# Linear attention and a bilinear FFN on one Trainium2 core: first stores over three queues, bulk loads and conversions reordered in the opening

## The chip, the core and the metric

The kernel runs on one NeuronCore of one Trainium2 chip. A core has TensorE (matmuls, results in PSUM), VectorE, ScalarE, GpSimd and SyncE, each with an instruction stream of its own that runs in program order, and 16 DMA engines that are fed through queues. SyncE, ScalarE and GpSimd can all issue DMAs. The metric is the device time of one execution in microseconds (us); the kernel before has a median of 604.79 us over 4 runs (604.5 to 605.08).

## What is computed

The reference has two stages. The first is a gated linear attention over 4 batches, 8 heads, 768 tokens and 48 channels; the second is a bilinear feed-forward block over its 3072 tokens of 384 channels:

```python
f = 1.0 / (1.0 + np.exp(-f_logit))
for t in range(S):
    state = f[:, :, t, :, None] * state + np.einsum('bhd,bhe->bhde', k[:, :, t], v[:, :, t])
    y[:, :, t] = np.einsum('bhd,bhde->bhe', q[:, :, t], state)
...
a = x @ w_a
b = x @ w_b
return (a * b @ w_out).astype(np.float32)
```

x is y with its heads side by side. w_a and w_b are 384 x 1536 and w_out is 1536 x 384; all three come as 64-bit floats, the rest as 32-bit.

## The kernel before

**Units and blocks.** The attention is done in 16 units. A unit is one batch, one half of its tokens (384) and four heads; units 0 and 1 are the two head groups of the first half of batch 0, units 2 and 3 those of its second half. Two units make one block of 384 tokens, whose y, turned so that channels lie on partitions, is the tile xT (three channel tiles of 128, numbered by kt). Unit 0 of a block fills channels 0 to 191, unit 1 the rest, so each unit's y goes to xT in five DMAs (`stores_of`, L533 to L556), since heads of 48 channels straddle the tiles of 128. Three sets of input tiles serve the units in turn (`sets[u % 3]`).

**One unit.** `front_parts` (L296 to L341) turns the gates into running products: two sigmoids on ScalarE (L306, L309), an affine step on GpSimd (L312), then on VectorE two scans of f (L316), a check (`hold`, L319), a reciprocal (L324), six scans of the inverse (L329), and the products of k and q with them (L333). Then come, on TensorE, `scores` (L387), `turn` (transposes of k, L411), `within` (L484), `gains` (L435) and `across` (L505); on VectorE `mask` (L400), five or six `carry` steps (L462, L464) and, in a first half, `hand_on` (L473). `within` and `across` add y up in two PSUM banks; `out_of_bank` (L514 to L524) copies it to SBUF in three parts: one copy for bank 0 and two, of 48 rows each, for bank 1. `stored` issues the five DMAs and, from unit 2 on, the loads of the unit three further on.

**Weights.** The weights are loaded in 20 pieces (`load_weights`, L239), most of 768 KB, and each is turned to 32 bits by `from_double` (L52): ScalarE L58 and L59, GpSimd L60, ScalarE L62 and L63, VectorE L68 and L73. `begin(n)` issues the ScalarE and GpSimd part up to piece n - 1 (half a piece for n.5), `end(n)` VectorE's; from the third piece on, `end` also issues a further piece's load where a buffer comes free. Pieces are counted from 0 here. There are four raw buffers, used in turn, and two early ones.

**The feed-forward block.** `up(blk, ft)` (L578 to L602) multiplies xT of a block with 128 columns of w_b and w_a: for each, channel tiles 0, 1, 2 in turn, six matmuls of 128 x 384, which the trace shows as twelve since a 32-bit matmul is two. `product` (L604) copies b out of PSUM on ScalarE (L610), multiplies on VectorE (L612) and gives the two banks back; there are four such banks.

**Order.** The opening, units 0 to 3 and up(0, 0) to up(0, 4), is written out by hand (L935 to L1064), and each engine runs its instructions in this order. Then follow up(0, 5), up(1, 0) and so on, in a loop that converts the remaining pieces as it goes (L1067 to L1077). From L1080 on a planner lays the steps of the remaining units and of the FFN side by side by costs and due times. The change lies in the opening alone. SyncE issues the loads and most stores there; of the stores of units 0 and 1, unit 0's first two and unit 1's last two are on ScalarE's queue (L545).

**Semaphores of DMAs.** The DMAs of SyncE and ScalarE share eight semaphores; a DMA waits until the one that used its semaphore before has landed. In the trace the stores of units 0 and 1 wait in this way too.

Of the kernel before, what the change touches and what calls it, by code (L numbers as in the profile page):

```python
# [26 lines left out]
R = 64  # L27
SUB = 64
# [108 lines left out]
def by_quotients(ctx, tc, q, k, f_logit, v, moe_w_a, moe_w_b, moe_w_out, out, ident, weights, bad):  # L137
    nc = tc.nc
    B, H, D, S = q.shape
# [4 lines left out]
    NQ = H // 4  # L144
# [7 lines left out]
    FIRST = range(NQ)  # L152
# [46 lines left out]
    def load_unit(u, names="fkqv"):  # L199
        for do in loads_of(u, names):  # L200
            do()
# [37 lines left out]
    def load_weights(n=1):  # L239
        for _ in range(n):  # L240
            if len(raws) == len(todo):
                return
            dst, src, (k, m) = todo[len(raws)]
            raw = dst
            if src.dtype != FP32:

                if len(raws) in EARLY:
                    raw = groups[:, EARLY.index(len(raws))].bitcast(mybir.dt.uint64)
                else:
                    raw = next(raw_places)  # L250
                raw = raw[:, 0:k * m].rearrange("p (k m) -> p k m", k=k)
            nc.sync.dma_start(out=raw, in_=src)
            raws.append(raw)
# [16 lines left out]
    def end(n):  # L270

        while ended[0] < min(n, len(todo)):
            begin(ended[0] + 1)
            next(going[ended[0]], None)
            ended[0] += 1
            if ended[0] > 2 and ended[0] - 1 not in EARLY:
                load_weights()
# [15 lines left out]
    def halves(x):  # L293
        return x.rearrange("p n s -> p (n s)")
# [48 lines left out]
    def front(u):  # L343

        for part in front_parts(u):
            for _, _, do, *args in part:
                do(*args)
            yield
# [5 lines left out]
    def tokens(n, c, p):  # L354

        return slice(n * BLK + c * C + p * SUB, n * BLK + c * C + p * SUB + SUB)

    def each():
        for n in range(2):
            for c in range(NC):  # L360
                yield n, c, (n * NC + c) * SUB
# [13 lines left out]
    def pair_of(x):  # L375

        return [x[:, i] for i in range(2)]

    def scores(u):
        t = sets[u % NSET]  # L380
        qf, kf = halves(t["q"]), halves(t["k"])
        ps = pair_of(home(u))
        for n, c, o in each():
            for h in range(2):
                for p in range(2):
                    r = slice(R * h, R * h + D)
                    nc.tensor.matmul(  # L387
                        ps[h][SUB * p:SUB * p + SUB, o:o + SUB],
                        lhsT=kf[r, tokens(n, c, p)],
                        rhs=qf[r, tokens(n, c, p)],  # L390
                        start=True,
                        stop=True,
                    )
# [9 lines left out]
    def turn(u):  # L403

        kf = halves(sets[u % NSET]["k"])
        live.setdefault(u, {})["kT"] = sb1.tile([128, 2, NC, 128], FP32, tag="kT", name="kT")
        ps = live[u]["turned"] = [ps_f[idle.pop(0)] for _ in range(2)] if u in FIRST else pair_of(away(u))
        for n in range(2):
            for c in range(NC):
                o = n * BLK + c * C  # L410
                nc.tensor.transpose(ps[n][:, c * C:c * C + C], kf[:, o:o + C], ident)  # L411
# [36 lines left out]
    def carried(u, js=range(NJ)):  # L448

        for j in js:  # L450
            if j + 1 < len(live[u]["st"]):
                carry(u, j)
        if js[-1] == NJ - 1:
            give_back(live[u]["turned"])
# [11 lines left out]
    def hand_on(u):  # L466

        if unit(u)[1] == NH - 1:
            return
        before = live[u]["st"][-1]  # L470
        for n in range(2):
            end = products_of_f[u][:, n, BLK - 1:BLK]
            nc.vector.tensor_scalar(before[:, n], before[:, n], end, math.exp(-MIDDLE), ALU.mult, ALU.mult)  # L473

    def within(u):

        t, at = sets[u % NSET], live[u]["at"]
        ps = live[u]["y"] = pair_of(home(u) if u < 2 * NQ else ps_y)
        for n, c, o in each():
            for p in range(2):  # L480
                for h in range(2):
                    r = slice(SUB * p, SUB * p + SUB)
                    e = R * (p ^ h)
                    nc.tensor.matmul(  # L484
                        ps[p][e:e + D, o:o + SUB],
                        lhsT=t["v"][r, n, c, h * D:h * D + D],
                        rhs=at[r, h, o:o + SUB],
                        start=o == 0,
                        stop=True,
                        skip_group_check=True,  # L490
                    )

    def across(u):

        b, half, qd = unit(u)
        qf, st, ps = halves(sets[u % NSET]["q"]), live[u]["st"], live[u]["y"]

        for n, c, o in reversed(list(each())) if half or u in FIRST else each():
            for p in reversed(range(2)) if u in FIRST else range(2):
                j = 2 * c + p  # L500
                if j == half == 0:
                    continue
                for h in range(2):
                    r, e = slice(R * h, R * h + D), R * (p ^ h)
                    nc.tensor.matmul(  # L505
                        ps[p][e:e + D, o:o + SUB],
                        lhsT=st[j][r, n],
                        rhs=qf[r, tokens(n, c, p)],
                        start=False,
                        stop=True,  # L510
                        skip_group_check=True,
                    )

    def out_of_bank(u, part):  # L514

        if not part:
            if u == NQ - 1:

                live[u]["y_sb"] = groups[:, 2 * NTG - 1, PIECE:].rearrange("r (o p m) -> r o p m", p=2, m=SUB)
            else:  # L520
                live[u]["y_sb"] = sb1.tile([128, 2 * NC, 2, SUB], FP32, tag="y", name="y")
        p, e, r, rows = ((0, 0, 0, 128), (1, R, 0, D), (1, 0, R, D))[part]
        copy = nc.vector.tensor_copy if u in FIRST and part > u else nc.scalar.copy
        copy(live[u]["y_sb"][r:r + rows, :, p], live[u]["y"][p][e:e + rows, 0:BLK].rearrange("r (o m) -> r o m", m=SUB))  # L524

    def stored(u):
# [6 lines left out]
    def stores_of(u):  # L533

        b, half, qd = unit(u)
        blk = b * NH + half

        def begin():
            if qd == 0:
                xT[blk] = sb2.tile([128, NKT, BLK], FP32, tag="xT", name="xT")  # L540
            live.pop(u - NQ, None)

        def store(n, h, kt, p, row, w):
            y = live[u]["y_sb"].rearrange("r (n c) p m -> r n (c p m)", n=2)
            queue = nc.scalar if u in FIRST and n == u else nc.sync  # L545
            queue.dma_start(out=xT[blk][p:p + w, kt], in_=y[row:row + w, n])

        yield begin
        for n in range(2):
            for h in range(2):  # L550
                ch, row, left = (4 * qd + 2 * n + h) * D, R * h, D
                while left:
                    kt, p = divmod(ch, 128)
                    w = min(left, 128 - p)
                    yield partial(store, n, h, kt, p, row, w)
                    ch, row, left = ch + w, row + w, left - w  # L556
# [378 lines left out]
    with tc.manual_schedule():  # L935
# [6 lines left out]
                eng.memset(sets[u][n], 30.0 if n == "f" else 0.0)  # L942
        for ps in (ps_x, ps_y):
            nc.scalar.copy(ps[:, :, 0:BLK], zero.unsqueeze(1).broadcast_to((128, 2, BLK)))
        fronts = [front(u) for u in range(2 * NQ)]

        def y_of(u):
            for part in range(3):
# [15 lines left out]
        load_weights(2)  # L964
        load_unit(2, "k")
        load_unit(2, "q")
        load_unit(2, "v")
        load_unit(3, "f")
        load_weights()
        for _ in range(3):  # L970
            next(fronts[0])
        begin(1)
# [8 lines left out]
        turned(1)  # L981
        mask(0)
        scores(1)
        next(fronts[2])
        begin(2.5)
        carried(0, range(4))
        within(0)
# [3 lines left out]

        carried(1, range(1))
        carried(0, range(4, 5))
        within(1)
        gains(1, range(NC - 1, NC))
        across(0)
# [9 lines left out]
        end(2)  # L1006
        for u in FIRST:
            carried(u, range(5, NJ))
            hand_on(u)


        load_unit(3, "k")
        load_unit(3, "q")
        load_unit(3, "v")
        load_weights()
        up(0, 0)
        for _ in range(3):
            next(fronts[2])
        begin(4)
        next(fronts[3])  # L1020
        end(4)
        turn(2)
        scores(2)
        load_unit(4, "f")
# [14 lines left out]
        across(2)  # L1039
        end(6)  # L1040
        y_of(2)
        load_weights()
        turn(3)
        turned(3)
        scores(3)
        begin(7)
        product()
        up(0, 3)
        mask(3)
        begin(7.5)  # L1050
# [4 lines left out]
        begin(8)  # L1055
        up(0, 4)
        end(8)
        across(3)
        y_of(3)
        load_unit(4, "k")  # L1060
        load_unit(4, "q")
        load_unit(4, "v")
        load_weights()
        product()  # L1064


# [534 lines left out]
```

## Time and profile before

| what | value |
|---|---|
| median of 4 runs | 604.79 us (604.5 to 605.08) |
| the profiled execution's own time | 605.34 us |
| its span, first to last instruction | 603.6 us |
| TensorE busy | 567.4 us (94%) |
| VectorE busy | 412.2 us (68%) |
| ScalarE busy | 268.4 us (44%) |
| GpSimd busy | 75.4 us (12%) |
| mean granted TensorE clock | 0.986 |
| DMA, mean over the span | 82 GB/s |

The profile page gives busy time by engine, then 40 slices of the span as tenths, then groups of instructions. PE is TensorE, PEld its weight loads, DVE VectorE, ACT ScalarE, POOL GpSimd, SP SyncE; a q behind the name is the engine's sequencer, which issues DMAs and waits. Numbers with L are lines of the kernel. In the timeline the columns are start and length in us, engine, line, operation, what is written and read, the shape and the count; in brackets stands how long the engine was idle before and what ended that. The windows view gives, for stretches of time, each engine's busy time and count of instructions, the granted clock (1.00 is full speed), the share of the DMA engines in use and the rate. The DMA view gives the size of a transfer and the time from its issue to its landing.

### The profile page before, as it was taken

What the parts mean: (1) busy time and instruction counts of PE and PEld (TensorE: products, weight loads), DVE (VectorE), ACT (ScalarE), POOL (GpSimd) and SP (SyncE); (2) the same over time, 40 slices, a digit from 0 to 9 for tenths busy, and PEclk for the clock granted to TensorE, in tenths of its full rate; (3) what the DMA queues carried; (4) which work ended last, traced back from release to release, by engine and by line L of the source; (5) the groups of instructions that cost most, each with busy time, mean ns of one, the idle gap of its engine ahead of it and who ended that gap; (6) DMA issues with size and microseconds to landing.
All of it is one profiled execution on the core that took longest, in us unless ns stands there. A gap on an engine that the chain in (4) does not pass through costs nothing.

```text
span 603.6 us, 13889 instructions
## 1 busy us (share of the span) xinstructions
PE 567.4 (94%) x5778; PEld 509.3 (84%) x5778; DVE 412.2 (68%) x787; ACT 268.4 (44%) x506; POOL 75.4 (12%) x69
## 2 busy tenths in 40 slices
PE   1578899999999999999999999999999999999995
PEld 1545455557899999999999999999999999999995
DVE  6797444589968778967895768846775165746741
ACT  6567779963132455326521354326331335134300
POOL 6233245534200000000000000000000000000000
PEclk9869999999999999999999999999999999999999
DMA  9963997059743232045003420032001100000000
GB/s 212 259 217 90 273 276 246 16 93 170 143 127 105 77 87 63 2 106 119 3 1 90 111 52 2 1 92 55 2 2 47 47 0 1 2 27 0 1 29 31
DMA packets 33336, 49.42 MB, mean 82 GB/s; under 512 B 3952, under 2 KB 25072, under 8 KB 33264
## 3 DMA queue, kind: packets, MB, share of 16 engines
q1 hardware_dynamic: 30016, 42.38, 25.8%
q0 software_dynamic: 2992, 5.77, 5.7%
q8 instruction: 47, 0.77, 0.6%
q10 hardware_dynamic: 256, 0.30, 0.2%
q14 instruction: 25, 0.20, 0.1%
HBM read 33.23 MB, written 4.72 MB: 63 GB/s over the span
## 4 chain that ended last, share of the span: by engine, by line
PE 84%; DVE 8%; ACT 3%; issue 2%; DMA 1%; SPq 0%; DVEq 0%; ACTq 0%
PE ps_f L712 35%; PE ps_f L805 27%; PE ps_f L590 14%; PE ps_y L484 2%; PE ps_y L505 2%; PE ps_x L387 2%; DVE sums L704 1%; DVE inv L329 1%; PE ps_x L435 1%; PE ps_x L411 1%; DVE groups L704 1%; DVE q_in L333 1%; DVE at L400 1%; DMA f_in<-in_f_logit_dram 1%; DVE groups L316 1%
## 5 line engine op out<-in xcount | busy, mean ns | idle before, releaser
L590 PE MATMUL ps_f<-xT,w_ba 128*128 128x384 f32 x288 | 98.9, 501 | 7.3 <-DMA xT<-y 6.3
L590 PEld LDWEIGHTS ps_f<-xT,w_ba 128*128 128x128 f32 x288 | 55.0, 195 | 46.3 <-DMA xT<-y 7.1
L1249 ACT COPY sums<-ps_f 128x384 f32<-128x384 f32 x120 | 57.5, 480 | 75.9 <-PE ps_f L712 68.2
L1249 ACT COPY groups<-ps_f 128x384 f32<-128x384 f32 x120 | 57.7, 481 | 62.9 <-PE ps_f L712 39.9
L712 PE MATMUL ps_f<-xT,w_ba 128*128 128x192 f32 x384 | 78.4, 327 | 0.0
L712 PEld LDWEIGHTS ps_f<-xT,w_ba 128*128 128x128 f32 x384 | 64.8, 190 | 0.2
L712 PE MATMUL ps_f<-groups,w_ba 128*128 128x192 f32 x288 | 55.4, 327 | 0.0
L712 PE MATMUL ps_f<-x_sums,raw 128*128 128x192 f32 x288 | 54.0, 331 | 1.2 <-DVE groups L704 0.9
L805 PE MATMUL ps_f<-w_out,sums 128*128 128x192 f32 x288 | 52.1, 329 | 0.0
L805 PE MATMUL ps_f<-w_out,groups 128*128 128x192 f32 x288 | 51.7, 328 | 0.0
L712 PEld LDWEIGHTS ps_f<-x_sums,raw 128*128 128x128 f32 x288 | 46.9, 190 | 4.3 <-DVE groups L704 1.8
L805 PE MATMUL ps_f<-spare,sums 128*128 128x192 f32 x288 | 49.0, 326 | 0.0
L712 PEld LDWEIGHTS ps_f<-groups,w_ba 128*128 128x128 f32 x288 | 47.9, 190 | 0.5 <-ACT groups L1249 0.3
L805 PEld LDWEIGHTS ps_f<-w_out,sums 128*128 128x128 f32 x288 | 47.1, 190 | 0.7 <-DVE o L840 0.3
L805 PEld LDWEIGHTS ps_f<-w_out,groups 128*128 128x128 f32 x288 | 47.1, 190 | 0.7
L60 POOL TENSOR_SCALAR sums<-sums 128x768 f32<-128x768 f32 (+1 forms) x20 | 40.0, 2001 | 58.4 <-ACT sums L58 58.3
L805 PEld LDWEIGHTS ps_f<-spare,sums 128*128 128x128 f32 x288 | 47.1, 190 | 0.1
L312 POOL TENSOR_SCALAR inv<-inv 128x768 f32<-128x768 f32 x14 | 12.6, 903 | 266.8 <-ACT inv L309 266.7
L704 DVE TENSOR_TENSOR sums<-sums,groups 128x768 f32<-128x768 f32 x36 | 34.7, 964 | 14.2 <-ACT groups L1249 13.7
L704 DVE TENSOR_TENSOR sums<-ps_f,sums 128x384 f32<-128x384 f32 x60 | 32.8, 553 | 16.5 <-PE ps_f L712 15.1
L712 PE MATMUL ps_f<-x_sums,w_ba 128*128 128x192 f32 x192 | 39.3, 327 | 0.5 <-DVE sums L704 0.5
L712 PE MATMUL ps_f<-xT,raw 128*128 128x192 f32 x192 | 39.4, 328 | 0.0
(134 smaller groups left out, 852.7 us busy)
## 6 DMA issues: line engine op xcount, KB each, us to landing
raw<-w_ba POOLq DMA_DIRECT2D x11, 512.0 KB, 8.3
k_in<-in_k_dram SPq DMA_DIRECT2D x32, 144.0 KB, 3.5
q_in<-in_q_dram SPq DMA_DIRECT2D x32, 144.0 KB, 4.1
v_in<-in_v_dram SPq DMA_DIRECT2D x16, 288.0 KB, 5.0
raw<-in_moe_w_out_dram SPq DMA_DIRECT2D x6, 768.0 KB, 4.2
out_dram<-o SPq DMA_DIRECT2D x24, 192.0 KB, 1.9
f_in<-in_f_logit_dram SPq DMA_DIRECT2D x28, 144.0 KB, 2.9
xT<-y SPq DMA_DIRECT2D x43, 72.0 KB, 2.2
```

Source lines behind the costliest of these rows:

```text
L60: nc.gpsimd.tensor_scalar(h, h, HI_MAX, None, ALU.min)
L312: nc.gpsimd.tensor_scalar(inv, inv, EXP_K, 1.0, ALU.mult, ALU.add)
L316: nc.vector.tensor_tensor_scan(F[:, c], F[:, c], none, math.exp(MIDDLE), ALU.mult, ALU.add)
L329: nc.vector.tensor_tensor_scan(inv[:, w], inv[:, w], none[:, 0:C], first, ALU.mult, ALU.add)
L387: nc.tensor.matmul(ps[h][SUB * p:SUB * p + SUB, o:o + SUB], lhsT=kf[r, tokens(n, c, p)], rhs=qf[r, tokens(n, c, p)], start=True, stop=True,)
L484: nc.tensor.matmul(ps[p][e:e + D, o:o + SUB], lhsT=t["v"][r, n, c, h * D:h * D + D], rhs=at[r, h, o:o + SUB], start=o == 0, stop=True, ski ...
L505: nc.tensor.matmul(ps[p][e:e + D, o:o + SUB], lhsT=st[j][r, n], rhs=qf[r, tokens(n, c, p)], start=False, stop=True, skip_group_check=True,)
L590: nc.tensor.matmul(ps[nm][:, 0:BLK], lhsT=w[:, kt, ft * 128:ft * 128 + 128], rhs=xT[blk][:, kt], start=kt == 0, stop=kt == NKT - 1,)
L704: nc.vector.tensor_tensor(to, x, y, op)
L712: nc.tensor.matmul(ps[:, g], lhsT=sums_of_w[name][:, g, 128 * j:128 * j + 128], rhs=sums_of_x[blk][name], start=start and g == 0, stop=Tru ...
L805: nc.tensor.matmul(to, lhsT=x[:, i // 2, i % 2], rhs=w[:, NI * (i % 2) + i // 2], start=start and i == 0, stop=i == HFT - 1, skip_group_ch ...
L1249: do(*args)
```

## The change

The diff, whole but for its file names:

```diff
@@ -495,21 +495,26 @@
         b, half, qd = unit(u)
         qf, st, ps = halves(sets[u % NSET]["q"]), live[u]["st"], live[u]["y"]
 
-        for n, c, o in reversed(list(each())) if half or u in FIRST else each():
-            for p in reversed(range(2)) if u in FIRST else range(2):
-                j = 2 * c + p
-                if j == half == 0:
-                    continue
-                for h in range(2):
-                    r, e = slice(R * h, R * h + D), R * (p ^ h)
-                    nc.tensor.matmul(
-                        ps[p][e:e + D, o:o + SUB],
-                        lhsT=st[j][r, n],
-                        rhs=qf[r, tokens(n, c, p)],
-                        start=False,
-                        stop=True,
-                        skip_group_check=True,
-                    )
+        order = [(n, c, o, p) for n, c, o in each() for p in range(2)]
+        if u in FIRST:
+
+            order = sorted(order[::-1], key=lambda x: -x[3])
+        elif half:
+            order = [(n, c, o, p) for n, c, o in reversed(list(each())) for p in range(2)]
+        for n, c, o, p in order:
+            j = 2 * c + p
+            if j == half == 0:
+                continue
+            for h in range(2):
+                r, e = slice(R * h, R * h + D), R * (p ^ h)
+                nc.tensor.matmul(
+                    ps[p][e:e + D, o:o + SUB],
+                    lhsT=st[j][r, n],
+                    rhs=qf[r, tokens(n, c, p)],
+                    start=False,
+                    stop=True,
+                    skip_group_check=True,
+                )
 
     def out_of_bank(u, part):
 
@@ -520,7 +525,7 @@
             else:
                 live[u]["y_sb"] = sb1.tile([128, 2 * NC, 2, SUB], FP32, tag="y", name="y")
         p, e, r, rows = ((0, 0, 0, 128), (1, R, 0, D), (1, 0, R, D))[part]
-        copy = nc.vector.tensor_copy if u in FIRST and part > u else nc.scalar.copy
+        copy = nc.vector.tensor_copy if u in FIRST and p else nc.scalar.copy
         copy(live[u]["y_sb"][r:r + rows, :, p], live[u]["y"][p][e:e + rows, 0:BLK].rearrange("r (o m) -> r o m", m=SUB))
 
     def stored(u):
@@ -542,7 +547,7 @@
 
         def store(n, h, kt, p, row, w):
             y = live[u]["y_sb"].rearrange("r (n c) p m -> r n (c p m)", n=2)
-            queue = nc.scalar if u in FIRST and n == u else nc.sync
+            queue = nc.sync if u != NQ - 1 else nc.gpsimd if n else nc.scalar
             queue.dma_start(out=xT[blk][p:p + w, kt], in_=y[row:row + w, n])
 
         yield begin
@@ -942,7 +947,11 @@
                 eng.memset(sets[u][n], 30.0 if n == "f" else 0.0)
         for ps in (ps_x, ps_y):
             nc.scalar.copy(ps[:, :, 0:BLK], zero.unsqueeze(1).broadcast_to((128, 2, BLK)))
-        fronts = [front(u) for u in range(2 * NQ)]
+        fronts = {u: front(u) for u in (0, 1, 3)}
+
+        def emit_all(steps):
+            for _, _, do, *args in steps:
+                do(*args)
 
         def y_of(u):
             for part in range(3):
@@ -964,9 +973,6 @@
         load_weights(2)
         load_unit(2, "k")
         load_unit(2, "q")
-        load_unit(2, "v")
-        load_unit(3, "f")
-        load_weights()
         for _ in range(3):
             next(fronts[0])
         begin(1)
@@ -981,7 +987,7 @@
         turned(1)
         mask(0)
         scores(1)
-        next(fronts[2])
+        emit_all(front_parts(2)[0])
         begin(2.5)
         carried(0, range(4))
         within(0)
@@ -991,6 +997,8 @@
 
         carried(1, range(1))
         carried(0, range(4, 5))
+        _, (first_scan, *scans), *others = front_parts(2)
+        emit_all([first_scan])
         within(1)
         gains(1, range(NC - 1, NC))
         across(0)
@@ -1006,19 +1014,23 @@
         end(2)
         for u in FIRST:
             carried(u, range(5, NJ))
-            hand_on(u)
-
-
+        emit_all([*scans, *others[0]])
+
+
+        load_unit(3, "f")
+        load_unit(2, "v")
+        load_weights()
         load_unit(3, "k")
         load_unit(3, "q")
         load_unit(3, "v")
         load_weights()
         up(0, 0)
-        for _ in range(3):
-            next(fronts[2])
+        emit_all(others[1])
         begin(4)
         next(fronts[3])
         end(4)
+        for u in FIRST:
+            hand_on(u)
         turn(2)
         scores(2)
         load_unit(4, "f")
@@ -1039,12 +1051,12 @@
         across(2)
         end(6)
         y_of(2)
-        load_weights()
+        load_weights(2)
         turn(3)
         turned(3)
         scores(3)
+        product()
         begin(7)
-        product()
         up(0, 3)
         mask(3)
         begin(7.5)
@@ -1055,12 +1067,12 @@
         begin(8)
         up(0, 4)
         end(8)
+        begin(9)
         across(3)
         y_of(3)
         load_unit(4, "k")
         load_unit(4, "q")
         load_unit(4, "v")
-        load_weights()
         product()
```

What it does:

- `across` of units 0 and 1 works through bank 1 first and then bank 0; before, the two alternated. For units 2 and later the order stays.
- `out_of_bank` copies both parts of bank 1 on VectorE for units 0 and 1; before, unit 1's first such part was on ScalarE.
- Unit 0's five stores go on SyncE, unit 1's first three on ScalarE and its last two on GpSimd.
- The loads of v of unit 2, f of unit 3 and weight piece 4 move from ahead of the first stores to behind them. f of unit 3 goes first of these; GpSimd clears its tile beforehand (L214).
- Unit 2's VectorE work is issued in three pieces: one scan of f ahead of `within(1)`, the second scan to the inverse scans behind the last carries of units 0 and 1, the two products behind up(0, 0). `hand_on` of units 0 and 1 moves behind `end(4)`.
- Behind `y_of(2)` two weight pieces are loaded instead of one, and the single one behind the loads of unit 4 goes: piece 9 moves there, pieces 10 and 11 take the places of 9 and 10.
- The `product` of up(0, 2) moves ahead of `begin(7)`.
- `begin(9)`, which is the ScalarE and GpSimd part of piece 8, is new ahead of `across(3)` and `y_of(3)`; before, this was issued behind up(0, 5).

## The prediction

> **What bounds the kernel now.** I read the page first, then the timeline of the first 125 us, the idle time before each TensorE instruction, the windows view for the granted clock, and the DMA view narrowed to single transfers.
>
> From the page, busy tenths and clock in 40 slices of 15 us:
> ```profile
> PE   1578899999999999999999999999999999999995
> PEclk9869999999999999999999999999999999999999
> ```
> TensorE is full from the sixth slice on; all that it lacks lies in the first five, as does the low clock. From the timeline, where y of units 0 and 1 becomes the first xT:
> ```profile
> 28.49 0.48 ACT L524 COPY groups<-ps_y 128x384 f32<-128x384 f32 x1 [1.95 <-PE ps_y L505]
> 29.48 0.55 DVE L524 COPY groups<-ps_y 48x384 f32<-48x384 f32 x1 [1.74 <-ACT groups L524]
> 31.79 1.87 SPq L546 DMA_DIRECT2D xT<-y  x3
> 33.75 1.65 PE L590 MATMUL ps_f<-xT,w_ba 128*128 128x384 f32 x2 [5.31 <-DMA xT<-y]
> 33.76 1.80 SPq L546 DMA_DIRECT2D xT<-groups  x3
> 36.34 5.68 PE L590 MATMUL ps_f<-xT,w_ba 128*128 128x384 f32 x10 [0.94 <-DMA xT<-groups]
> ```
> y is out of the bank at 30.03, SyncE starts its stores only at 31.79, issues six in a row (0.54 to 0.60 each) and the last lands at 36.9: TensorE stands idle 5.31 and 0.94 us. The windows view (columns: stretch, length, PE busy, PEld, DVE, ACT, POOL, clock, DMA share, GB/s) shows what that costs beyond the idle time:
> ```profile
> 20.30:23.70 3.40, 3.12 (x124) 2.85 (x113) 3.16 (x10) 3.37 (x6) 1.29 (x2) 0.51 1.06 255
> 27.10:30.50 3.40, 0.76 (x32) 0.61 (x32) 1.56 (x5) 0.95 (x2) 0.00 (x0) 1.00 0.93 283
> 30.50:33.90 3.40, 0.15 (x1) 0.15 (x1) 3.33 (x11) 2.63 (x4) 0.00 (x0) 0.51 0.35 102
> 33.90:37.30 3.40, 2.46 (x4) 1.04 (x5) 3.33 (x10) 3.37 (x5) 2.12 (x1) 0.50 0.35 90
> 37.30:40.70 3.40, 3.40 (x7) 1.84 (x6) 3.26 (x5) 1.60 (x4) 1.85 (x2) 0.50 0.79 207
> ```
> A stretch with 0.76 busy is followed by half clock; one with 2.46 doesn't bring it back, those with 3.12 and 3.40 do. At half clock a matmul half of L590 takes 0.64 us, at full clock 0.34 (12 in 4.07). The second place, units 2 and 3:
> ```profile
> 54.91 3.96 SPq L546 DMA_DIRECT2D xT<-y  x5
> 61.06 0.56 DVE L612 TENSOR_TENSOR groups<-ps_f,x_sums 128x384 f32<-128x384 f32 x1 [4.43 <-ACT x_sums L610]
> 62.54 0.89 PE L484 MATMUL ps_y<-at,v_in 64*48 64x64 f32 x48 [1.31 <-DVE at L400]
> 62.79 0.45 SPq L252 DMA_DIRECT2D raw<-in_moe_w_b_dram  x1
> 68.93 1.46 ACT L524 COPY y<-ps_y 128x384 f32<-128x384 f32 x3 [3.92 <-PE ps_y L505]
> 71.38 0.90 ACT L58 ACTIVATE sums<-raw 128x768 f32<-128x768 f32 x1
> 74.58 50.79 PE L590 MATMUL ps_f<-xT,w_ba 128*128 128x384 f32 x156 [1.02 <-DMA xT<-y]
> ```
> From 74.58 on no hole of TensorE is over 0.9 us, and the change leaves that part of the program as it is but for one piece's conversion. So the whole effect is read at one point: up(1,0), TensorE's first work on block 1, gets its third channel tile when unit 3's last store lands, 72.39 + 2.9 = 75.3. I call "lead" how much earlier the changed kernel reaches a place than this trace.
>
> **Part by part.** *First y.* The transfers of v(2), f(3) and weight piece 4 (1.3 MB) leave the queue ahead of the stores. SyncE's wait until 31.79 is for the landing of ScalarE's first store, slow (3.2 us instead of 1.9 to 2.2) because piece 4 was in flight until 31.4. Now unit 0's five stores go on SyncE as soon as VectorE's copies end (27.2 and 27.7, behind the carries that end at 26.6): five by 0.6 from 27.2, the third, which completes channel tile 0, lands at 28.4 + 1.9 = 30.3, the fifth at 31.5. Unit 1's bank with two copies is done after 24 of 40 matmuls (28.1 instead of 28.44), VectorE copies at 28.15 to 29.25 while ScalarE copies the other bank until 28.97; before, VectorE waited for ScalarE until 29.46. ScalarE then issues three stores (the last lands at 32.15), GpSimd two. *GpSimd's price* is not in this trace for such a store. From below: SyncE's 1.9 us. From above: its accumulating 512 KB transfers issue in 1.2 to 3.2 us, the first, with the queue empty, lands after 5.6. Those behind it land 2.7 apart, so 2.9 of the 5.6 doesn't grow with size; plus a seventh of 2.7 that is 3.3. I take 3.3: second store 30.2 + 3.3 = 33.5; bounds 32.1 and 35.8.
>
> Channel tile 0 starts at 30.4, tile 1 at 31.7, tile 2 at 33.5. The stretch 30.6 to 34.0 is then busy for 2.9 of 3.4, between the 2.46 that failed and the 3.12 that sufficed: up(0,0) ends at 36.4 (full clock from 34.0) or 38.0 (from 37.4) instead of 42.02.
>
> *VectorE.* Work from 28.15 up to the end of carried(2), by this trace's rows: two copies 1.1, piece 1 (L68, L73) 1.06, two carries 0.53, one scan 0.91 (the other now lies in the hole of 0.92 before the carries at 25.45, so at nothing; if it slips, 0.9 at most), hold to the last inverse scan 2.7, two products 2.1, pieces 2 and 3 3.5, hand_on 0.8 (moved behind them; it is due only at carried(2) and across(2)), mask 0.87, unit 3's scans 4.8, two L612 0.95, five carries 1.4: 20.7, so 48.9. TensorE reaches across(2) at 36.4 or 38.0 + 10.9 (42.02 to 52.94) = 47.3 or 48.9, against 52.94: **lead 4.0**, with VectorE as the next bound. f(3), v(2) and pieces 4 to 7 land later by order but are needed later than they land: SyncE waits for GpSimd's memset of f(3), behind both software stores, until 32.2; f(3) lands near 35.6, ScalarE reads it at 36.3.
>
> *product ahead of begin(7).* L610 no longer stands behind 3.5 us of conversion (57.04 to 60.6), so mask(3) is done before up(0,3) ends and the wait of 1.31 before L484 goes: lead 5.3. up(0,5) ends at 72.9 - 5.3 = 67.6.
>
> *begin(9) ahead of y(3).* ScalarE gets four more instructions ahead of unit 3's copies: L58 to L63 of piece 8, 3.55 us a piece (71.38 to 74.92). It idles there 3.92 us, so they look free. But L58 must have piece 8, which is still issued behind unit 2's stores and unit 5's seven loads. The DMA view narrowed to it:
> ```profile
> raw<-in_moe_w_b_dram SPq DMA_DIRECT2D x1, 768.0 KB, 6.8
> ```
> 62.79 + 6.8 = 69.5 in this trace, with DMA engines full (share 1.03 to 1.08 from 61 to 70). Its chain starts at y(2), so it keeps the lead of 4.0: 65.5. ScalarE is ready at 61, waits, converts until 69.1, and the three copies (1.46) end at 70.55, against 70.39 now. **Nothing of the lead of 5.3 is left at y(3).** Queued behind the waiting L58 are these copies, and behind them L610 of up(0,4), without which up(1,0) has no bank: VectorE frees it at 71.6.
>
> *Two pieces instead of one behind y(2).* Piece 11 is now issued ahead of unit 3's stores. Pieces land 2.0 to 3.1 apart; 8 to 11 are in by about 72.2 (74.11 - 4.0 + 2.1). Here the first store took 4.4 us behind such a piece. In the changed kernel the stores are issued from 70.1 to 72.55, the last lands at 72.55 + 1.9 = 74.45, against 75.3: **0.8 us gained.**
>
> *The clock.* TensorE idles from 67.6 to 71.6, 4 us, so by the rows above the next stretch is at half clock. The clock changed in this trace only at 20.3, 23.75, 30.6, 40.8, all multiples of 3.41 apart. On that grid full clock is back at 74.95, as the stretch is busy but for some 0.4 us; cost (74.95 - 74.45)/2 = 0.3. Off it, up to 3.4 us later: 1.9.
>
> **Sum:** -0.8 + 0.3 = -0.5. The profiled execution took 605.34 (span 603.6, 1.7 around it), 0.55 above the median of 604.79; both move by the same: 604.3.
>
> *The skill against this.* The Trainium skill, DMA: Bandwidth & Descriptors, "Issuing engines are not separate DMA queues", says that several issuing engines save only sequencer time, usually small beside the transfer. By it the three queues bring next to nothing and only the freed queue counts. Here the six issues took 3.8 us against 1.9 for a landing, so the row speaks for the saving. TensorE: Matmul & The Clock Gate, Part 1, calls the clock's window free-running; by that the grid differs from run to run, and the clock's cost would be an estimated 1.1 rather than 0.3, the sum +0.3.
>
> **Rivals.** (1) *More lead, piece 8 sooner.* q's product took 1.58 us beside GpSimd's work where others take 0.95, and hold 0.76 instead of 0.16: without both VectorE's chain is 1.2 shorter. Piece 8 landed 3.1 us behind v(5), while piece 9 took 2.0: 1.05 more. All three: 604.3 - 2.25 = 602.1. The stores can't land before piece 11, so much below 601 isn't to be had.
> (2) *Slower: GpSimd's second store.* Up to 34.2 or so lead 4.0 shrinks to 3.5, which the sum of -0.5 just bears. Later than that each us costs one us: at the upper bound, 35.8, the clock stays at half until 40.8, up(0,0) ends at 40.9, lead 1.1: 604.3 + 2.9 = 607.2. For it: no small software store in the trace, and 3.2 us issues seen. Against: GpSimd is idle from 25.4 to 34.0.
> (3) *The copies don't overlap.* If VectorE's copies of one bank wait for ScalarE's of the other, as they did for the same bank (1.74 idle above), y(1) is out at 30.15, GpSimd's second store lands at 34.1 and the clock stays low until 37.4: lead 2.5 to 3.4, some 605.5. The part then doesn't do what it says.
>
> **Numbers.** Forecast 0.50 (603.0 to 606.0), (1) 0.22, (2) 0.16, (3) 0.12. 0.2%, about what a measurement here can tell, is 1.2 us: under 603.6 lie (1) and a fifth of the forecast, 0.32; over 606.0 (2) and parts of (3) and of the clock's cost, 0.23; 0.45 between. The range leaves a tenth out on each side: 602.0 to 606.8.
>
> **What would show it.** Right: tile 2 of up(0,0) near 33.5, across(2) near 49, L58 of piece 8 waiting on its DMA at 65 and unit 3's L524 behind it near 69, TensorE idle some 4 us before up(1,0), then half clock. Wrong: L524 of unit 3 at 63 to 65 (then 2 to 4 us faster), a store of GpSimd over 5 us, or any new hole after 76 us.

## The result, and the profile after

The changed kernel took 607.24 us (median of 43 runs, 604.07 to 609.64), the kernel before in the same sessions 604.95 (64 runs, 603.75 to 608.62). The ratio is 1.0032, 95% interval 1.0024 to 1.0039: **slower by 0.3%**, where 604.3 was forecast. The profiled execution took 607.22 (span 605.5) against 605.34 (603.6).

In the page of the kernel after, the two rows that answer to those of before:
```profile
PE   1688899999999999999999999999999999999995
PEclk9978999999999999999999999999999999999998
```
TensorE is busier in the second and third slice (15 to 45 us), and the PE row nowhere shows what was lost. The clock is better in these two slices and worse in the fourth (8 instead of 9). TensorE's instructions, laid beside those of before one by one, give it: the first matmul of `across(2)` is 2.6 us earlier (50.36 against 52.94), that of `across(3)` 2.3 us earlier (65.69 against 67.95), and from 78 us on, but for 157 to 164 us, all are 1.35 us later, up to the last matmul (598.33 against 596.98). A gain of 2.3 us turns into a loss of 1.35 within some 15 us. Another 0.5 us lies behind the last matmul (7.2 us to the end of the span instead of 6.6), outside what the change touches; the traces of the runs below have 6.6 to 6.8 or 7.0 to 7.2 there, faster and slower kernels in both groups.

The opening, in the timeline of after (columns as before: start, length, engine, line, operation; in brackets the idle time before and what ended it):
```profile
26.91 1.14 DVE L529 COPY y<-ps_x 48x384 f32<-48x384 f32 x2 [0.34 <-ACT y L529]
27.50 4.06 SPq L551 DMA_DIRECT2D xT<-y  x5
28.18 0.48 ACT L529 COPY groups<-ps_y 128x384 f32<-128x384 f32 x1 [1.30 <-PE ps_y L510]
28.69 1.14 DVE L529 COPY groups<-ps_y 48x384 f32<-48x384 f32 x2 [0.64 <-ACT groups L529]
29.56 1.33 POOL L551 DMA_DIRECT2D xT<-groups  x2 [3.76 <-DVE groups L529]
32.84 0.98 PE L595 MATMUL ps_f<-xT,w_ba 128*128 128x384 f32 x1 [4.71 <-DMA xT<-y]
```
SyncE starts to store at 27.50 instead of 31.79, as meant, yet TensorE's first matmul on xT comes at 32.84 against 33.75. VectorE's copies of bank 1 waited for ScalarE's of bank 0, for both units.

The second place, in the timeline of after:
```profile
52.86 0.87 PE L411 MATMUL ps_x<-ident,k_in 128*128 128x128 f32 x6 [1.61 <-ACT y L529]
54.52 5.83 PE L595 MATMUL ps_f<-xT,w_ba 128*128 128x384 f32 x12
60.28 0.89 PE L484 MATMUL ps_y<-at,v_in 64*48 64x64 f32 x48
65.87 0.93 ACT L58 ACTIVATE sums<-raw 128x768 f32<-128x768 f32 x1 [3.44 <-DVE w_ba L73]
66.51 4.14 PE L595 MATMUL ps_f<-xT,w_ba 128*128 128x384 f32 x12
69.43 1.44 ACT L529 COPY y<-ps_y 128x384 f32<-128x384 f32 x3
70.40 3.06 SPq L551 DMA_DIRECT2D xT<-y  x5
71.42 0.91 PE L595 MATMUL ps_f<-xT,w_ba 128*128 128x384 f32 x2 [0.78 <-ACT x_sums L615]
72.96 0.88 PE L595 MATMUL ps_f<-xT,w_ba 128*128 128x384 f32 x2 [0.63 <-DMA xT<-y]
75.17 4.18 PE L595 MATMUL ps_f<-xT,w_ba 128*128 128x384 f32 x7 [1.32 <-DMA xT<-y]
```
The wait of 1.31 ahead of L484 is gone. Unit 3's copies, which could start just behind the end of `across(3)` at 66.58, start at 69.43: in front of them on ScalarE stands L58 of piece 8, which waited 3.44 us. (The releaser the row names is not the last one. Piece 8 itself landed at 65.79.) The three holes in the last rows are TensorE's, in up(1, 0): the first ends when a bank comes free, behind the `product` that stands after these copies on ScalarE, the other two when the second and the third channel tile land. The windows view of after shows what they cost (columns as before):
```profile
68.31:71.72 3.41, 2.63 (x9) 1.35 (x8) 0.32 (x1) 3.32 (x8) 0.70 (x1) 1.00 0.56 206
71.72:75.14 3.42, 1.50 (x4) 0.30 (x3) 0.70 (x2) 3.39 (x5) 2.13 (x1) 1.00 0.38 101
75.14:78.55 3.41, 3.38 (x6) 1.89 (x7) 0.00 (x0) 0.64 (x2) 0.00 (x0) 0.50 1.03 237
```
After the stretch with 1.50 us busy comes one at half clock, in which TensorE, always busy, does half the work: 1.7 us lost. Unit 3's last store lands at about the same time in both kernels (75.03 and 75.33); the half clock behind it makes the rest.

### The profile page after: what moved, and what is told of

Its sections match the earlier page's. It is cut to its first block, busy times and chain, and to the rows that moved or that the text cites. A ratio compares the mean times of both kernels' runs of the same rounds, so it can differ in the third digit from the quotient of the medians.

```text
span 605.5 us, 13891 instructions
## 1 busy us (share of the span) xinstructions
PE 571.6 (94%) x5778; PEld 511.7 (85%) x5778; DVE 411.8 (68%) x788; ACT 268.4 (44%) x505; POOL 77.3 (13%) x71
## 4 chain that ended last, share of the span: by engine, by line
PE 83%; DVE 8%; DMA 3%; issue 2%; ACT 2%; SPq 1%; DVEq 0%; ACTq 0%
PE ps_f L717 35%; PE ps_f L810 27%; PE ps_f L595 14%; PE ps_y L510 2%; PE ps_x L387 2%; PE ps_y L484 1%; DVE sums L709 1%; DVE inv L329 1%; PE ps_x L411 1%; PE ps_x L435 1%; DMA raw<-in_moe_w_b_dram 1%; DMA xT<-y 1%; DVE groups L709 1%; DVE q_in L333 1%; DVE f_in L316 1%
## 5 line engine op out<-in xcount | busy, mean ns | idle before, releaser
L595 PE MATMUL ps_f<-xT,w_ba 128*128 128x384 f32 x288 | 101.8, 512 | 7.4 <-DMA xT<-y 6.7
L595 PEld LDWEIGHTS ps_f<-xT,w_ba 128*128 128x128 f32 x288 | 56.3, 199 | 48.1 <-issue 13.2
L717 PEld LDWEIGHTS ps_f<-xT,w_ba 128*128 128x128 f32 x384 | 64.8, 190 | 0.2
L617 DVE TENSOR_TENSOR groups<-ps_f,x_sums 128x384 f32<-128x384 f32 x24 | 13.2, 553 | 39.5 <-PE ps_f L595 16.4
```

What stands on the lines that cost most here:

```text
L595: nc.tensor.matmul(ps[nm][:, 0:BLK], lhsT=w[:, kt, ft * 128:ft * 128 + 128], rhs=xT[blk][:, kt], start=kt == 0, stop=kt == NKT - 1,)
L617: nc.vector.tensor_tensor(products(blk)[:, :, ft], a, b, ALU.mult)
L717: nc.tensor.matmul(ps[:, g], lhsT=sums_of_w[name][:, g, 128 * j:128 * j + 128], rhs=sums_of_x[blk][name], start=start and g == 0, stop=Tru ...
```

## The experiments

All ratios are to the kernel before on the same chip. A table first, since the cause shows across the kernels; "bulk" is the last weight piece that SyncE issues ahead of unit 3's stores. Times in us in each kernel's own trace.

| kernel | ratio [95%] | bulk landed | unit 3's first store issued, landed | last landed | half clock behind it |
|---|---|---|---|---|---|
| before | 1 | 74.11 | 69.92, 74.33 | 75.33 | 0 |
| after | 1.0032 [1.0024, 1.0039] | 72.07 | 70.40, 72.50 | 75.03 | 3.41 |
| x1, no begin(9) | 1.0040 [1.0028, 1.0052] | 73.87 | 66.73, 74.09 | 74.96 | 6.83 |
| k5, x1 with ScalarE's queue | 1.0029 [1.0013, 1.0046] | 74.03 | 67.41, 73.82 | 75.09 | 3.41 |
| k7, begin(9), loads as before | 1.0029 [1.0010, 1.0048] | 70.55 | 71.15, 73.22 | 75.90 | 3.41 |
| x3, before with both tail edits | 1.0071 [1.0052, 1.0089] | 74.83 | 72.81, 75.07 | 77.45 | 3.41 |
| x4, opening alone | 0.9962 [0.9950, 0.9974] | 70.60 | 67.20, 70.80 | 71.91 | 0 |
| m1, two pieces ahead | 0.9987 [0.9974, 1.0000] | 67.15 | 67.22, 69.30 | 71.87 | 0 |
| m2, before with bulk moved | 0.9946 [0.9926, 0.9965] | 70.25 | 67.95, 70.44 | 72.66 | 0 |

Two different things end the wait of unit 3's y, and either is enough. Where the stores are issued early, the first lands within 0.25 us of the bulk (before, x1, k5, x4, m2). Where ScalarE holds them (after, k7, x3), it lands 2.1 to 2.3 us behind its issue, and the last 2.4 to 2.7 us behind the first, at the pace of their issue.

### x1: without begin(9) ahead of across(3)

```diff
-        begin(9)
         across(3)
```


> The changed kernel without begin(9) ahead of y(3); everything else as changed. Theory A (ScalarE's conversion of piece 8 holds unit 3's copies, and the hole that this makes brings the half clock): copies of unit 3 start when across(3) ends, near 66.6 instead of 69.4, the stores land just behind piece 11 (72.1), the third channel tile of up(1,0) starts near 73 instead of 75.2, the hole ahead of it is under 2 us and no half clock follows: some 4 us below the changed kernel, 603 (0.3% below the kernel before). Theory B (the loss comes from the opening: three queues and the half clock at up(0,3)): within 0.5 us of the changed kernel, near 607.

Measured: 607.41 us (606.54 to 608.6, 6 runs), no gain. Timeline of x1, unit 3's copies, stores and the first matmul that needs them:
```profile
65.74 1.46 ACT L529 COPY y<-ps_y 128x384 f32<-128x384 f32 x3 [2.49 <-PE ps_y L510]
66.73 3.06 SPq L551 DMA_DIRECT2D xT<-y  x5
74.44 15.76 PE L595 MATMUL ps_f<-xT,w_ba 128*128 128x384 f32 x40 [4.08 <-DMA xT<-y]
```
The copies come 3.7 us sooner, the stores too, and they take 5.8 to 7.4 us each. The DMA view of x1, narrowed to them and to piece 11 (kind, size, time from issue to landing):
```profile
xT<-y SPq DMA_DIRECT2D x3, 72.0 KB, 6.2
```
```profile
raw<-in_moe_w_a_dram SPq DMA_DIRECT2D x1, 768.0 KB, 11.7
```
Piece 11 was issued at 62.17 and landed at 73.87. The theory that ScalarE's wait alone holds y(3) fell here: with that wait gone, the second piece behind `y_of(2)` holds the stores for as long.

### x2 and x4: without either tail edit

```diff
         y_of(2)
-        load_weights(2)
+        load_weights()
...
         load_unit(4, "v")
+        load_weights()
         product()
```
That, on top of x1, is x2. x4 also puts `product()` back behind `begin(7)`, so that it is the change's opening and nothing else.

> As x1_no_begin9, and the weight loads as before too: one piece behind y(2), one behind unit 4's loads, so that only three pieces lie ahead of unit 3's stores. Theory A: the stores are then bound by their own issue, the last lands near 72.1 instead of 73, 0.5 to 1 us below x1_no_begin9: 602. If piece 11 ahead of the stores doesn't matter (rival): the same as x1_no_begin9. Theory B: near 607.

> The opening alone: the changed kernel with the loads of pieces 8 to 11, begin(9) and the place of the product of up(0,2) as before. Theory A: the lead of 2.3 to 2.6 at across(2) stays, the 1.3 us wait for mask(3) is back, the stores land behind piece 10 near 72 to 73: 2 us below the kernel before, 603. Theory B: slower than before, 606 to 607.

Measured: x2 602.87 us (601.79 to 607.64, 10 runs), ratio 0.9966 [0.9954, 0.9979]; x4 602.29 (601.93 to 605.64, 12 runs). Timeline of x4:
```profile
66.21 1.46 ACT L529 COPY y<-ps_y 128x384 f32<-128x384 f32 x3 [4.20 <-PE ps_y L510]
67.20 3.06 SPq L551 DMA_DIRECT2D xT<-y  x5
71.14 19.16 PE L595 MATMUL ps_f<-xT,w_ba 128*128 128x384 f32 x58 [0.30 <-DMA xT<-y]
```
The hole of 4.08 is 0.30, and no half clock follows. The traced execution of x2 was its longest, 607.64 us, and shows the other outcome with the same order of loads:
```profile
66.35 3.06 SPq L551 DMA_DIRECT2D xT<-y  x5
73.84 2.90 PE L595 MATMUL ps_f<-xT,w_ba 128*128 128x384 f32 x4 [3.86 <-DMA xT<-y]
```
Piece 10 landed at 73.19 there and not at 70.60 as in x4, the first store right behind it at 73.50, and 6.83 us of half clock followed (72.76 to 79.59). So one late piece ahead of the stores is enough for the loss; why it was late in this execution stays open. The opening gains 0.4%; the two tail edits cost 0.7%. `product` ahead of `begin(7)` changes nothing that can be measured (0.9966 against 0.9962).

### x3 and k7: the tail edits on the kernel before, and begin(9) alone

x3 is the kernel before with `load_weights(2)` behind `y_of(2)`, none behind unit 4's loads, and `begin(9)` ahead of `across(3)`. k7 is the changed kernel with the loads of x2.

> The kernel before with the two late edits alone: two pieces behind y(2) and none behind unit 4's loads, and begin(9) ahead of across(3). Theory A: without the opening's lead piece 8 lands at 69.5, the copies of unit 3 start at 73.1 instead of 68.9, the last store lands near 79, TensorE stands idle over 5 us and gets half clock for up to 3.4 us: 3.7 + 1.7 = 5 us slower than before, 610. Theory B: within 1 us of the kernel before.

> The changed kernel with begin(9) kept ahead of y(3), but the weight loads as before (one piece behind y(2), one behind unit 4's loads). Theory C with both holds (conversion and queue each hold unit 3's stores until about the same time): copies from 69.4 as in the changed kernel, the stores no longer wait behind a piece but are issued from 70.4, the last lands at 74.5 to 75: 606 to 607.5, little gained. Rival (only the queue matters): 603.

Measured: x3 609.29 us (607.43 to 611.25), k7 606.84 (606.21 to 608.95, 11 runs). Timeline of k7:
```profile
66.65 0.91 ACT L58 ACTIVATE sums<-raw 128x768 f32<-128x768 f32 x1 [4.11 <-DMA raw<-in_moe_w_b_dram]
70.19 1.43 ACT L529 COPY y<-ps_y 128x384 f32<-128x384 f32 x3
71.15 3.07 SPq L551 DMA_DIRECT2D xT<-y  x5
72.18 3.21 PE L595 MATMUL ps_f<-xT,w_ba 128*128 128x384 f32 x4 [3.15 <-ACT x_sums L615]
```
Here no bulk is left when the stores are issued (piece 10 landed at 70.55), and the y is late because ScalarE waited 4.11 us for piece 8 and then converted it. x1 and k7 each remove one of two holds and gain nothing; x2 removes both and gains 0.7% (1.0032 to 0.9966).

### k5: unit 3's stores on ScalarE's queue

```diff
-            queue = nc.sync if u != NQ - 1 else nc.gpsimd if n else nc.scalar
+            queue = nc.scalar if u == 3 else nc.sync if u != NQ - 1 else nc.gpsimd if n else nc.scalar
```
On x1, with the product of up(0, 4) moved ahead of `y_of(3)`, so that it isn't queued behind the stores.

> x1_no_begin9 with unit 3's five stores issued by ScalarE instead of SyncE (and the product of up(0,4) ahead of unit 3's copies, so that it isn't held by these issues). Bulk, order and time of the copies stay. Theory C (the stores wait in SyncE's queue behind the last piece): the stores land 2 to 3.2 us after their issue, from 69.5 to 73 instead of 74.1 to 75, TensorE waits under 2.5 us and keeps full clock: 603.5. Rival (the DMA engines are busy, whatever the queue): they land with piece 11 near 74 and the time stays near 607.

Measured: 607.0 us (606.46 to 608.44, 11 runs). The DMA view of k5 around its stores, then that of x4:
```profile
xT<-y ACTq DMA_DIRECT2D x3, 72.0 KB, 5.6
xT<-y ACTq DMA_DIRECT2D x1, 48.0 KB, 6.0
```
```profile
xT<-y SPq DMA_DIRECT2D x3, 72.0 KB, 2.4
xT<-y SPq DMA_DIRECT2D x1, 48.0 KB, 2.8
```
From a queue of its own a store still takes 5.6 us and lands with the bulk (73.82 against 74.03 for piece 11): what was issued earlier on another queue goes first here. The place to wait is the DMA engines, not SyncE's queue. The windows view of k5, from the first issue to ScalarE's first packet and then around the first landings, shows two parts of the wait:
```profile
67.40:70.00 2.60, 2.60 (x10) 1.54 (x9) 0.00 (x0) 0.47 (x1) 0.00 (x0) 1.00 1.04 386
73.00:74.50 1.50, 0.12 (x1) 0.15 (x1) 0.00 (x0) 1.47 (x3) 1.03 (x1) 0.92 0.10 28
```
Up to 70.0 all 16 engines are full, and all 507 packets in this stretch are from SyncE's queue. From 73.0 to 74.5, while the first stores and the piece land, only 0.10 of the engines' time is in use, as much as one or two of the 16 would take. So the end of the wait isn't for the rate of all sixteen; it looks like a few that lag, which this view can't name. The Trainium skill, DMA: Bandwidth & Descriptors, "Issuing engines are not separate DMA queues", says that transfers from all issuing engines run on the same 16 DMA engines and that several issuers save only the issue time; k5 agrees, with 5.6 us.

### k6: TensorE kept busy in the hole

```diff
             up(blk, i)
+            for _ in range(5 if n == 0 else 0):
+                nc.tensor.matmul(ps_x[:, 0, 0:BLK], lhsT=w_b[:, 0, 0:128], rhs=xT[0][:, 0], start=True, stop=True)
             end(7 + n)
```
On x1: five matmuls into a bank nobody reads at that time, between up(0, 5) and up(1, 0).

> x1_no_begin9 with five matmuls of 128x384 between up(0,5) and up(1,0) that write a bank that is free there and whose result nobody reads (3.4 us of the 4.1 us hole; added work, nothing left out). Theory C (a hole of 4 us brings 3.4 to 6.8 us of half clock behind it): the hole shrinks to about 0.6 us, up(1,0) starts at the same time and the half clock behind it goes: 607.4 - 3.4 = 604. Rival (the half clock doesn't hang on the hole, or the hole alone is the cost): 607 or above.

Measured: 605.66 us (604.34 to 608.05, 11 runs), ratio 1.0008 [0.9988, 1.0029] against 1.0040 for x1: 0.3%, some 1.9 us (the two intervals, from two chips, just touch). The windows view of k6, then that of x1 where the clock fell:
```profile
70.90:74.30 3.40, 3.40 (x11) 1.82 (x10) 0.00 (x0) 3.37 (x5) 1.92 (x2) 1.00 0.56 133
74.30:77.70 3.40, 3.40 (x12) 1.88 (x11) 0.13 (x1) 1.90 (x3) 1.05 (x1) 1.00 0.94 219
```
```profile
72.91:76.33 3.42, 1.89 (x3) 1.17 (x4) 0.00 (x0) 2.39 (x3) 1.88 (x1) 0.50 0.54 145
76.33:79.74 3.41, 3.41 (x7) 1.73 (x6) 0.00 (x0) 0.48 (x1) 0.00 (x0) 0.50 1.05 224
```
The clock stays full when the hole is filled with work of no use, so the half clock comes from the hole. Of the 3.4 us that two windows at half clock seemed to cost, 1.9 came back: in the first of them TensorE had only 1.89 us of work, and part of it was a wait for data anyway. The size that was expected was too large, the mechanism holds.

### k8: bank 1 copied first

```diff
-            for part in range(3):
+            for part in (1, 2, 0):
                 out_of_bank(u, part)
```
On x4, for units 0 and 1. (The branch that makes the tile y goes with whichever part comes first.)

> x4_opening_alone with the copies of units 0 and 1 written in the order bank 1, bank 1, bank 0, so that VectorE's two come ahead of ScalarE's in the program. If VectorE waited because its copies come second on the same tile of y: it now starts 0.6 to 0.9 us sooner, ScalarE's copy comes last, the stores start some 0.4 us sooner: 0.2 to 0.4 us below x4_opening_alone, 602. If the wait was for something else: the same starts as in the changed kernel and no difference.

Measured: 603.68 us (602.37 to 604.18, 11 runs), ratio 0.9967 [0.9950, 0.9984], no gain over x4. Timeline of k8:
```profile
28.16 0.48 ACT L529 COPY y<-ps_x 128x384 f32<-128x384 f32 x1 [3.50 <-DVE y L529]
28.38 1.12 DVE L529 COPY groups<-ps_y 48x384 f32<-48x384 f32 x2 [0.31 <-PE ps_y L510]
29.59 0.48 ACT L529 COPY groups<-ps_y 128x384 f32<-128x384 f32 x1 [0.95 <-DVE groups L529]
```
Now ScalarE waits for VectorE. The copies of one y run one after the other in the order of the program, whatever bank they read. A y with a tile for each bank, which might let them overlap, wasn't tried.

### m2, m3 and m4: the parts of the opening

m2 is the kernel before with only the three bulk loads moved:
```diff
         load_unit(2, "q")
-        load_unit(2, "v")
-        load_unit(3, "f")
-        load_weights()
...
+        load_unit(3, "f")
+        load_unit(2, "v")
+        load_weights()
         load_unit(3, "k")
```
m3 is x4 with the stores back on two queues (`queue = nc.scalar if u in FIRST and n == u else nc.sync`). m4 is x4 with the three bulk loads back where the kernel before has them.

> The kernel before, with nothing but the three bulk loads (unit 3's f, unit 2's v, piece 4) moved behind the stores of units 0 and 1. The kernel with the whole opening measured 602.29 us. Theory A (the bulk ahead of the stores was what held them, the queues, the order of the bank and the scans are small): the stores land by about 33.5 us, and the time is 602.3 to 603.3 us. Rival B (the three queues or the bank finished early carry a good share): 603.7 to 605 us, with TensorE's wait for xT at about 34 us or later.

> The opening alone, with its stores back on the two queues of the kernel before (unit 0's first half and unit 1's second on ScalarE's, the rest on SyncE's). Theory A (the queue sets only the issue, and the three land at about the same time): 602.3 us, within 0.6 of the opening alone. Rival B (the third queue takes two issues of 0.7 to 1.5 us off the chain): kt2 lands 1 us later, up(0, 0) ends 1 us later, and the time is 603.3 us or more. Rival C (GpSimd's stores, which take 2.9 us from issue to landing against 1.9 to 2.8 elsewhere, are the late ones): 601.5 us or less.

> The opening alone, with the three bulk loads back ahead of the stores as in the kernel before; the queues, the order of the banks and unit 2's scans stay as changed. Theory A (the bulk ahead is what held the stores): the gain of the opening is gone, 604.3 to 605.3 us, and the stores land behind piece 4. Rival B (queues, banks and scans carry a good share): 602.8 to 603.8 us.

Measured: m2 602.41 us (602.16 to 602.92, 6 runs), ratio 0.9946 [0.9926, 0.9965]; m3 602.18 (601.34 to 603.11, 6 runs), 0.9944 [0.9924, 0.9964]; m4 606.21 (604.13 to 608.72, 12 runs), 1.0006 [0.9989, 1.0023]. Timelines, m2 first:
```profile
27.49 2.97 SPq L546 DMA_DIRECT2D xT<-y  x3
31.72 1.62 PE L590 MATMUL ps_f<-xT,w_ba 128*128 128x384 f32 x2 [3.92 <-DMA xT<-y]
```
and m4:
```profile
27.73 0.77 SPq L252 DMA_DIRECT2D groups<-in_moe_w_b_dram  x1
28.59 7.92 SPq L551 DMA_DIRECT2D xT<-y  x5
36.67 1.62 PE L595 MATMUL ps_f<-xT,w_ba 128*128 128x384 f32 x2 [6.45 <-DMA xT<-y]
```
Within what these runs can tell, some 0.2%, the bulk's place is the whole gain. With it, the queues of before give as much as three (m3, and m2's last store lands at 33.71, after's at 34.26); without it, queues, banks and scans give nothing that can be measured. TensorE even starts on the first tile sooner with two queues, at 31.57 in m3 against 32.83 in x4, where all five stores of unit 0 stand behind one another on SyncE.

### m1: only two pieces ahead of unit 3's y

x2 without any load behind `y_of(2)` and with `load_weights(2)` behind unit 4's loads.

> The changed kernel without the piece begun ahead of across(3), without any load behind y_of(2), and with two pieces loaded behind unit 4's k, q and v instead; the product of piece 7 stays where the change put it. Theory A (what holds unit 3's stores is the bulk that is issued ahead of them, two pieces in the changed kernel and one in the kernel with the loads as before): now pieces 8 and 9 alone stand ahead, so the stores land as soon as their own issue lets them, about 71.3 us (0.9 behind the last issue at 70.3 as in the kernel with the opening alone), the hole ahead of kt0 to kt2 is below 0.5 us, and no window of the clock is halved behind it: 602.0 us (601.3 to 602.9). Rival B (pieces 10 and 11, which now start only at about 70 us, are late for their conversions and matmuls in up(1, 1) or up(0, 6), and TensorE waits there): 603 to 605 us, with a hole behind 80 us that a DMA of w_b or w_a ended.

Measured: 604.63 us (603.66 to 606.07, 12 runs), ratio 0.9987 [0.9974, 1.0000]. The stores landed early, as theory A has it, but the time is rival B's: the bill comes at 88 us. Timeline of m1:
```profile
71.92 14.46 PE L595 MATMUL ps_f<-xT,w_ba 128*128 128x384 f32 x44 [0.42 <-DMA xT<-y]
83.91 0.90 ACT L58 ACTIVATE sums<-raw 128x768 f32<-128x768 f32 x1 [6.69 <-DMA raw<-in_moe_w_b_dram]
87.95 2.52 PE L595 MATMUL ps_f<-xT,w_ba 128*128 128x384 f32 x7 [1.58 <-ACT x_sums L615]
```
Piece 10, now issued behind twelve transfers of units 6 and 4 and landing at 83.88, is converted too late: ScalarE's product stands behind it and TensorE waits 1.58 us. Of none, one and two pieces behind `y_of(2)` (m1 0.9987, x2 0.9966, x1 1.0040), one, as before the change, came out best.

So the best versions, better than both kernels, are x4, m2 and m3, 602.2 to 602.4 us, which these runs can't tell apart. m2 is three lines.

## Why the prediction was wrong

**The step that failed is the clock's term:** "+0.3" in "-0.8 + 0.3 = -0.5". It measured +1.7. The -0.8 beside it measured about -0.3 (last store at 75.03 against 75.33), so the sum is +1.4, and the last matmul is 1.35 us late. The profiled executions differ by 1.9, with the 0.5 behind the last matmul; the medians differ by 2.3, and no trace shows the other 0.4.

Why the clock's term failed: I had TensorE idle from 67.6 to 71.6 and then busy "but for some 0.4 us", so that the half window would coincide with waiting. Measured, up(0, 5) ends at 70.65, since of the lead of 5.3 that put its end at 67.6 only 2.25 was there. The idle time is 2.73 and not 4, in pieces of 0.78, 0.63 and 1.32: up(1, 0) waits for its bank (until 71.42; forecast 71.6) and then for the second and the third channel tile. The window of the idle time ends at 75.14, and the half clock falls on 75.14 to 78.55, when all data is there. The grid itself was nearly where I set it (74.95), by chance, as shown below; the hole had moved on it. The estimate of 1.1 that stands beside the 0.3, for a grid that differs from run to run, makes the sum +0.3, which has the right sign, and the upper bound of 1.9 for this term covers the 1.7.

These are figures of one execution. Over all runs on record the mean granted clock is 0.9855 for the changed kernel (45 runs) and 0.9878 for the kernel before (76 runs of the experiments' sessions): 0.0023 of 605 us is 1.4 us, of the size of the 1.7. It is a rough measure only, since half clock during a wait costs little: m2, one of the fastest, has 0.9865.

Step by step:

- *Stores freed by the bulk's move:* right, and by m2 and m4 all that matters in the opening. The times were too early: the first tile was complete at 32.71 (forecast 30.3), the second at 34.26 (31.5) and the third at 33.92 (33.5). So the last to land was unit 0's fifth store on SyncE, on the queue I took to be the quick one. I counted 0.6 us an issue and 1.9 to land. SyncE's second issue took 1.47 (28.18 to 29.65), and the landings took 2.3 to 3.3.
- *Copies side by side:* wrong. They are serial, as rival 3 and k8 have it, and y(1) is out at 29.83 and not 29.25. Rival 3's lead of 2.5 to 3.4 fits the measured 2.6 by luck, though: it rests on GpSimd's second store landing at 34.1, which landed at 33.30, ahead of unit 0's last.
- *GpSimd's price* 3.3, bounds 1.9 to 5.6 behind the issue: measured 2.9 and 3.0. Its second store landed at 33.30, before SyncE's last. Rival 2 gave 607.2 by a late GpSimd; the time fits and the mechanism was not there.
- *Lead 4.0 at across(2):* measured 2.6. up(0, 0) ended at 39.44, and the 10.9 us from there to `across(2)`, taken from the trace of before, held to 0.02 us (50.36).
- *The wait ahead of L484 goes, lead +1.3:* right in itself. k7, with the same opening, reaches `across(3)` at 64.07, 3.9 us ahead of before. In the changed kernel's trace a hole of 1.61 at 52.86 fell so in its window that up(0, 3) ran at half clock, 5.83 us instead of 4.14, and took it back.
- *Nothing of the lead left at y(3):* right. Piece 8 forecast to land at 65.5, landed at 65.79; copies to end at 70.55, ended at 70.87. The landing is in part luck: y(2) was 2.6 us earlier and not 4.0, but SyncE took 1.3 us less from its first store of y(2) to the issue of piece 8 (6.58 against 7.88), which I hadn't counted.
- *Two pieces behind y(2), all in by 72.2:* measured 72.07, and for this kernel harmless, since ScalarE held the stores longer. As a bound on rival 1 it was drawn too loosely ("much below 601 isn't to be had"): in x1 piece 11 lands at 73.87 and takes all that 3.7 us of earlier copies could give.
- *The skill weighed against the change:* I took the issue of six stores (3.8 us) to speak for three queues. m3 shows that the page's rule was the better guide here: 0.9944 with two queues, 0.9962 with three, intervals overlapping.

What I should have asked is where the two tail edits would stand if the opening delivered all it could. Both tie unit 3's y to transfers that the opening can't bring forward as far.

## What to carry to other kernels

Put bulk loads behind a small store on which the next stage waits, on whatever queue: in these runs what was issued ahead of it landed ahead of it or with it. Before filling an engine's idle time with a step, see what the step itself waits for, since everything behind it in order then waits as well. When two holds end at about the same time, removing one alone measures as nothing; remove both before you call an edit harmless, and price the half-clock window that can come behind a hole.

## What the runs showed of the hardware

- A store of 72 KB took 2.2 us to land (median of SyncE's 45 in the page of after) and, behind 768 KB pieces, 6.2 from SyncE's queue (x1) and 5.6 from ScalarE's (k5), each the median of three.
- In the trace of after, stretches of 3.41 us with 1.50 and 1.80 us of TensorE work (the latter 51.25 to 54.66) are followed by half clock, one with 2.63 is not.
- The clock changes in steps of 3.41 us, but the grid isn't tied to the kernel's start: a change at 72.91 in x1 and one at 54.07 in x4 are 5.5 steps apart. The Trainium skill, TensorE: Matmul & The Clock Gate, Part 1, calls the window free-running, which these traces confirm. Which hole is punished is thus partly chance: behind the hole of 1.6 us at turn(3), x4 and the changed kernel have a half window, the kernel before, k7 and k8 have none.
- SyncE's second store issue took 1.4 to 1.9 us in the traces of after, x4, m2 and m3 (28.18 to 29.65 in after, 28.14 to 29.83 in m2), where most others take 0.6; in m2 and m3 ScalarE's second issue ended within 0.01 us of it. Why stays open.
